# A gated scan and top-1 MoE: the last two unconditional tiles' scatters stand behind the conditional parts

## The chip, the cores and the metric

The kernel runs on one core of a Trainium2 chip. The metric is the device time of one execution in microseconds (us). The engines are PE (matmuls; PEld is its weight load), DVE, ACT, POOL and SP. Here SP starts the loads and the gathers, POOL the indirect scatters. A "q" behind an engine's name (POOLq) means its sequencer: branches, semaphores, drains and the issue of DMAs.

## The reference

Four sequences of 5056 tokens with 256 channels go through a gated scan over time; the result, 20224 tokens, goes through a mixture of 8 experts, of which each token takes one.

```python
# B, S, D = 4, 5056, 256;  N = 20224;  E, F = 8, 1024
f = lower_bound + (1.0 - lower_bound) * sigmoid(f_logit)
for t in range(S):
    h = f[:, t] * h + (1 - f[:, t]) * x[:, t]
    y[:, t] = h
x = y.reshape(B * S, D)
e_idx = argmax(x @ w_gate, axis=1)
gate_w = softmax(x @ w_gate)[arange(N), e_idx]
eom = sigmoid(x @ w_output_gate)
for e in range(E):
    mask = e_idx == e
    ye = maximum(x[mask] @ w1[e], 0.0) @ w2[e]
    out[mask] = gate_w[mask, None] * eom[mask, e, None] * ye
```

## The kernel before

**Chunks.** The tokens go through the scan in 40 chunks of 512, channels on the partitions. `chunk()` is a generator; each `yield` ends a stage. In their order: the tanh on ACT (L265), (f - 1) x on DVE (L269), the scan on DVE (L280), squares on ACT (L287) and their sum on PE (`pv`, L291). From that sum `pow2` works out a power of two as a scale, in five DVE instructions on a 128x1 tile (L142, L144, L146, L148, L150: `xv`, `xs`, `xi`), each of which reads what the one ahead wrote; L296 and L299 make of it `sa` and `li`. With `sa` ACT writes the high f16 half of the result (L310) and DVE the low half (L314); SP turns both from channels to rows with transposing DMAs (L307), after which PE computes the gate logits (L329). The routing on DVE (L372 to L421: `oh`, `og`, `gs`, `pos`, `eg`) gives every token its place, and POOL scatters the rows, two f16 halves and the gate's factor, into `scr`, sorted by expert (L433).

**Weights.** The weights of each expert come in two halves, 16 in all. Each is loaded by SP (L566), bounded by a gram on PE (L578), a norm on DVE (L585) and a sum on PE (L592), scaled by the same five instructions of `pow2` (names with w), and split into a high half by ACT (L614) and a low one by DVE (L619, into `w1s` and `w2s`).

**First tiles.** While the weights arrive, 16 tiles of 128 rows, one per expert after chunk 3 and one after chunk 5, are gathered and computed (matmuls L715 to L717 and L735 to L737, relu on ACT, its low half `el` on DVE in L726). They use separate code because the expert is known in advance. What ends with the last of them, at about 184 us of the trace, is called the front part below.

**Tiles.** Then `experts()` computes tiles of sorted rows: 64 of 256 rows, and up to 37 more of 128 rows, as many as the routing has filled. 18 of the 37 always run, so that 82 tiles (0 to 81) are unconditional; the other 19 stand in two conditional parts, 3 behind `used > 18` and 16 behind `used > 21`. `used` is loaded in L964 from a count that the routing left; each `tc.If` (L966) becomes a branch on every engine. In the traced execution neither body runs.

A tile is gathered by SP with a transposing DMA (`xq`, L630) and a small load with its rows' factors and places (`mt`, L633). DVE copies the expert's first weights (L657), PE does the first product (L669 to L671), ACT the relu (L674), DVE the low half (L682), and PE the second product (L702 to L704). ACT writes the scaled result to `yo` (L746, two buffers), and `put` scatters it to the output with one indirect DMA on POOL per 128 rows (L750). The loop overlaps three tiles: in turn t it gathers tile t + 1, does the first product of t and the second of t - 1, and evacuates and scatters t - 2. At the border to the conditional parts the gather of the next tile (82) is issued ahead, in case they run. The chunks that are left run between the quarters of a tile, one stage at a time.

**Order.** The instructions are written in one program order, and the compiler's scheduler, which works with its own timeline, may move what does not depend on each other. `ordered(start, cut)` limits this: it walks the list and ties each instruction to the one ahead on the same engine. Instructions ahead of index `cut` on DVE, ACT, PE and POOL are left free; SP is always tied. The index `prog["cut"]` is taken where the front part ends.

```python
for i, ins in enumerate(nc.cur_bb.bb.instructions[start:]):
    free = i < cut and ins.engine in loose
    if ins.engine in prev and not free:
        tc.add_manual_dep(ins, prev[ins.engine], AFTER, reason="order")
    prev[ins.engine] = ins.name
```

So the front part is in SP's order as written, and in the scheduler's on the other four engines; all that follows stands as written. The program's end is L1003.

Of the kernel before, what the change touches and what calls it, by code (L numbers as in the profile page):

```python
# [8 lines left out]
F32 = mybir.dt.float32  # L9
# [3 lines left out]
I16 = mybir.dt.int16  # L13
# [32 lines left out]
def raw(ins):  # L46
    return getattr(ins, "ins", ins)
# [3 lines left out]
def tile_scan_moe(  # L51
# [11 lines left out]
    P = 128  # L63
    D, N = xT.shape
# [27 lines left out]
    gp = ctx.enter_context(tc.tile_pool(name="gp", bufs=3))  # L92
# [104 lines left out]
    def apart(ins, group, keep=()):  # L197
        tc.declare_no_dep(raw(ins), group=group, keep=[raw(k) for k in keep], reason="rows apart")
        tc.add_to_no_dep_group(group, raw(ins))
# [422 lines left out]
    mpool = {}  # L622

    def gather(t, slot, e=None):
        tab, j, nb, new = slot
        n = nb * P
        r = nc.sync.value_load(tab[j : j + 1, 0:1], min_val=0, max_val=FREE + P - n)
        xq = gp.tile([P, 2, KD, 256], I16, tag="xq", name="xq")
        mt = gp.tile([P, 2, 4], I16, tag="mt", name="mt", bufs=4)
        i1 = nc.sync.dma_start_transpose(  # L630
            out=xq.rearrange("p a k n -> p (a k) n")[:, :, 0:n], in_=scr[ds(r, n), 0 : 2 * D]
        )
        i2 = nc.sync.dma_start(out=mt[:, 0:nb, :], in_=scr[ds(r, n), CM : CM + 4].rearrange("(b p) d -> p b d", p=P))  # L633
        for ins in (i1, i2):
            for k in new:
                tc.add_manual_dep(raw(ins), raw(k).name, DATA, reason="rows scattered")
            apart(ins, "scr", new)
        return dict(xh=xq[:, 0].bitcast(F16), xl=xq[:, 1].bitcast(F16), mt=mt, nb=nb, tab=tab, j=j, id=t, ev=e)
# [100 lines left out]
    def evacuate(T):  # L739
        nb = T["nb"]  # L740
        if isinstance(T["ev"], int):
            T["yo"] = yo = ep.tile([P, 1, D], F32, tag="ey", name="ey", bufs=2)
        else:
            T["yo"] = yo = mpool["m"].tile([P, 2, D], F32, tag="yo", name="yo", bufs=2)
        for b in range(nb):
            nc.scalar.activation(yo[:, b, :], T["y"][:, b, :], AF.Copy, scale=T["fac"][:, b : b + 1])  # L746

# [6 lines left out]
            apart(ins, "out")  # L754


    prog = {"begun": 0, "tick": 0, "done": 0, "left": 0.0, "planned": 0, "final": False, "got": 0, "rounds": 0}
    live = []
    total = sure(N)
    tail = (N - 256 * total + E * (P - 1)) // P  # L760
# [54 lines left out]
    tiles = {}  # L815
# [95 lines left out]
    def ordered(start, cut):  # L911

        loose = [e.engine for e in (nc.vector, nc.scalar, nc.tensor, nc.gpsimd)]
        prev = {}
# [3 lines that stand above are left out]
                tc.add_manual_dep(ins, prev[ins.engine], AFTER, reason="order")  # L918
            prev[ins.engine] = ins.name

    def experts(t0, t1, more):
        ahead(t0)
        alone(expert(tiles[t0]))
        alone(fetch1(tiles[t0], 0))
        for t in range(t0, t1 + 2):
            T = tiles.get(t) if t < t1 else None
            U = tiles.get(t - 1) if t0 < t <= t1 else None
            V = tiles.get(t - 2) if t > t0 + 1 else None
            rate = RATE * (T or U or V)["nb"] / 2
            for q in range(4):  # L930
                tasks = []
                if q == 0:
                    if t + 1 < t1 + min(more, 1):
                        ahead(t + 1)
                    if T:
                        tasks.append(fetch1(T, 1))
                elif q == 2:
                    if t + 1 < t1:
                        alone(expert(tiles[t + 1]))
                        tasks.append(fetch1(tiles[t + 1], 0))  # L940
                elif q == 3 and T:
                    tasks.append(factors(T))
                if q == 0 and U:
                    tasks.append(low(U, 3))
                if q and T:
                    tasks.append(low(T, q - 1))
                step(rate, tasks)
                if q == 0 and V:
                    evacuate(V)
                if q == 1 and V:  # L950
                    put(V)
                if T:
                    gemm1(T, q)
                if U:
                    gemm2(U, q)

    cuts = [n for n in MORE if n < tail] + [tail]
    between["on"] = True
    experts(0, total + cuts[0], len(cuts) - 1)
    beside()  # L960
    ordered(0, prog["cut"])

    if len(cuts) > 1:
        used = nc.values_load(prog["count"][0:1, 0:1], min_val=0, max_val=tail)  # L964
        for a, b in zip(cuts[:-1], cuts[1:]):
            with tc.If(used > a):  # L966
                experts(total + a, total + b, 0)
                ordered(0, 0)


# [36 lines left out]
```

## Time and profile before

| | |
|---|---|
| time, median of 3 runs | 989.14 us (987.89 to 991.45) |
| time of the profiled execution | 990.77 us |
| its span / mean granted clock of PE | 989.1 us / 0.988 |
| busy: PE, DVE, ACT, POOL | 907.7, 801.0, 519.7, 390.1 us |
| first matmul of tile 0 (L669) | 184.5 us |

The span runs from the first to the last instruction of the profiled execution; 1.7 us of its time lie outside. Times in the rows are counted from the span's start. A row of the timeline has the start, the duration, the engine, line and operation with what it writes and reads, a count (x2: a second one follows), and in brackets the idle time ahead of it and what ended that. A row of a group ends with the idle time ahead of its instructions.

### The profile page before, as it was taken

How to read it: one execution, taken by the hardware profiler on the slowest of the kernel's cores; microseconds unless marked ns; L12 is line 12 of the kernel's file. 1: busy time of each engine (PE TensorE's matmuls, PEld its weight loads, DVE VectorE, ACT ScalarE, POOL GpSimd, SP SyncE). 2: the span in 40 equal slices, each digit the busy share in tenths (PEclk: the TensorE clock that was granted, in tenths of full speed). 3: DMA queues.
4: the chain of work that ended last, by engine and by line, in shares of the span. 5: the costliest groups of instructions: out<-in, count | busy, mean ns of one | idle time of the engine just before them, and what ended most of it. 6: DMA issues, size and time to landing. Idle time of an engine off the chain costs nothing. (4 is left out here: it accounts for less than half of the span.)

```text
span 989.1 us, 30907 instructions
## 1 busy us (share of the span) xinstructions
PE 907.7 (92%) x9775; PEld 819.7 (83%) x9775; DVE 801.0 (81%) x2639; ACT 519.7 (53%) x1075; POOL 390.1 (39%) x378
## 2 busy tenths in 40 slices
PE   2258898899999999999999999999999999999993
PEld 2247887788888888888888888888888888899992
DVE  7989897888989988888898888888888886545550
ACT  6667675555555555555565555555555543333331
POOL 1432334434445454454545434455444443211111
PEclk9999999999999999999999999999999999999997
DMA  8899984855575657556576665655666544312120
GB/s 310 206 275 293 237 230 126 188 157 151 131 157 144 151 153 167 141 133 152 150 153 150 169 138 140 153 148 157 150 163 134 129 100 90 100 45 43 41 57 17
DMA packets 238558, 146.56 MB, mean 148 GB/s; under 512 B 202557, under 2 KB 204223, under 8 KB 238400
## 3 DMA queue, kind: packets, MB, share of 16 engines
q1 hardware_dynamic: 222752, 101.74, 44.9%
q0 software_dynamic: 15360, 42.74, 14.4%
q8 instruction: 95, 1.56, 0.7%
q14 instruction: 63, 0.52, 0.2%
q10 hardware_dynamic: 288, 0.02, 0.0%
HBM read 58.38 MB, written 44.49 MB: 104 GB/s over the span
## 5 line engine op out<-in xcount | busy, mean ns | idle before, releaser
L674 ACT ACTIVATE hh<-ph 128x512 f16<-128x512 f32 (+1 forms) x328 | 180.4, 550 | 307.8 <-PE ph L671 297.4
L669 PE MATMUL ph<-xq,w 128*128 128x256 f16 (+1 forms) x1312 | 330.4, 260 | 2.9 <-DMA xq<-scr 2.4
L671 PE MATMUL ph<-xq,w 128*128 128x256 f16 (+1 forms) x1312 | 331.1, 261 | 0.0
L670 PE MATMUL ph<-xq,w 128*128 128x256 f16 (+1 forms) x1312 | 330.9, 261 | 0.0
L750 POOL DMA_INDIRECT out_dram<-yo,mt x146 | 175.3, 1201 | 363.2 <-ACT yo L746 339.9
L704 PE MATMUL py<-w2s,hl 128*128 x1168 | 318.5, 273 | 0.0
L703 PE MATMUL py<-w2s,hh 128*128 x1168 | 318.4, 273 | 0.0
L702 PE MATMUL py<-w2s,hh 128*128 x1168 | 318.1, 272 | 0.0
L682 DVE SCALAR_TENSOR_TENSOR hl<-ph,hh 128x512 f16<-128x512 f32 (+1 forms) x328 | 204.9, 625 | 58.2 <-ACT hh L674 55.8
L433 POOL DMA_INDIRECT scr<-rows,dst x154 | 175.7, 1141 | 122.6 <-issue 109.3
L657 DVE COPY w<-w1s 128x2048 f16 x164 | 120.3, 734 | 35.1 <-PE ph L671 33.3
L669 PEld LDWEIGHTS <-w 128*128 128x128 f16 x1312 | 127.9, 98 | 14.3 <-DVE fac L649 2.7
L671 PEld LDWEIGHTS <-w 128*128 128x128 f16 x1312 | 128.0, 98 | 11.9
L670 PEld LDWEIGHTS <-w 128*128 128x128 f16 x1312 | 127.9, 97 | 9.7
L704 PEld LDWEIGHTS <-hl 128*128 128x128 f16 x1168 | 114.1, 98 | 13.8
L702 PEld LDWEIGHTS <-hh 128*128 128x128 f16 x1168 | 114.0, 98 | 11.4
L703 PEld LDWEIGHTS <-hh 128*128 128x128 f16 x1168 | 113.9, 98 | 10.6
L280 DVE TENSOR_TENSOR_SCAN xt<-ft,xt 128x512 f32<-128x512 f32 (+4 forms) x78 | 90.8, 1172 | 0.0
L746 ACT ACTIVATE yo<-py,fac 128x256 f32<-128x256 f32 x146 | 61.8, 468 | 26.7 <-PE py L704 26.1
L314 DVE SCALAR_TENSOR_TENSOR ft<-xt,sa,ft 128x512 f16<-128x512 f32 (+1 forms) x76 | 56.2, 744 | 20.1 <-ACT ft L265 18.3
L329 PEld LDWEIGHTS <-ft 128*128 128x128 f16 x600 | 51.7, 99 | 15.1 <-ACT ft L310 4.9
L310 ACT ACTIVATE ft<-xt,sa 128x512 f16<-128x512 f32 (+1 forms) x76 | 50.2, 707 | 23.3 <-DVE li L299 16.0
(171 smaller groups left out, 1298.7 us busy)
## 6 DMA issues: line engine op xcount, KB each, us to landing
ft<-in_fT_dram SPq DMA_DIRECT2D x37, 512.0 KB
xt<-in_xT_dram SPq DMA_DIRECT2D x37, 512.0 KB
w<-in_wT_dram SPq DMA_DIRECT2D x32, 512.0 KB
scr<-rows,dst POOLq DMA_INDIRECT x154
rows<-ft SPq DMA_TRANSPOSE x152
out_dram<-yo,mt POOLq DMA_INDIRECT x146
xq<-scr SPq DMA_TRANSPOSE x99
scr<-padt SPq DMA_DIRECT2D x9, 136.0 KB
```

The lines of the kernel that those rows point to most:

```text
L280: nc.vector.tensor_tensor_scan(out=xt[:, k, a:z], data0=ft[:, k, a:z], data1=xt[:, k, a:z], initial=init, op0=ALU.mult, op1=ALU.add)
L433: ins = nc.gpsimd.indirect_dma_start(out=scr[:, :], out_offset=IOA(ap=dst[:, b : b + 1], axis=0), in_=rows[:, b, :], in_offset=None)
L657: nc.vector.tensor_copy(out=w, in_=w1f[:, ds(T["ev"] * (2 * WH) + h * 2 * QH, 2 * QH)])
L669: nc.tensor.matmul(out=o, lhsT=w[:, f, k, 0, :], rhs=T["xh"][:, k, 0:n], start=first, stop=False)
L670: nc.tensor.matmul(out=o, lhsT=w[:, f, k, 0, :], rhs=T["xl"][:, k, 0:n], start=False, stop=False)
L671: nc.tensor.matmul(out=o, lhsT=w[:, f, k, 1, :], rhs=T["xh"][:, k, 0:n], start=False, stop=last)
L674: nc.scalar.activation(hh[:, :, 0:n], ph[:, :, 0:n], AF.Relu)
L682: nc.vector.scalar_tensor_tensor(out=hl[:, :, 0:n], in0=ph[:, :, 0:n], scalar=0.0, in1=hh[:, :, 0:n], op0=ALU.max, op1=ALU.subtract)
L702: nc.tensor.matmul(out=o, lhsT=hh[:, i, c], rhs=wh, start=first, stop=False, skip_group_check=True)
L703: nc.tensor.matmul(out=o, lhsT=hh[:, i, c], rhs=wl, start=False, stop=False, skip_group_check=True)
L704: nc.tensor.matmul(out=o, lhsT=hl[:, i, c], rhs=wh, start=False, stop=last, skip_group_check=True)
L750: ins = nc.gpsimd.indirect_dma_start(out=out[:, :], out_offset=IOA(ap=T["mt"][:, b, 2:4].bitcast(I32), axis=0), in_=T["yo"][:, b, :], in_o ...
```

## The change

It has three parts.

- `mt` and `yo` of the conditional tiles get tags of their own (`mtc`, `yoc`; two buffers each).
- `experts` for the 82 unconditional tiles runs with `more` = 0: the gather of tile 82 is no longer issued ahead of the border.
- With `late` = 2 it leaves out `put` for tiles 80 and 81. They are scattered after both conditional parts, and a last `ordered(0, 0)` ties what now stands at the end of the block. Since it walks the block's whole list and with `cut` = 0, it also ties the front part's instructions on DVE, ACT, PE and POOL.

```diff
@@ gather
-        mt = gp.tile([P, 2, 4], I16, tag="mt", name="mt", bufs=4)
+        tag = prog["places"]
+        mt = gp.tile([P, 2, 4], I16, tag="mt" + tag, name="mt" + tag, bufs=2 if tag else 4)
@@ evacuate
-            T["yo"] = yo = mpool["m"].tile([P, 2, D], F32, tag="yo", name="yo", bufs=2)
+            tag = prog["places"]
+            T["yo"] = yo = mpool["m"].tile([P, 2, D], F32, tag="yo" + tag, name="yo" + tag, bufs=2)
...
-    def experts(t0, t1, more):
+    def experts(t0, t1, more, late=0):
...
-                if q == 1 and V:
+                if q == 1 and V and t - 2 < t1 - late:
                     put(V)
...
-    experts(0, total + cuts[0], len(cuts) - 1)
+
+    end = total + cuts[0]
+    late = min(2, end) if len(cuts) > 1 else 0
+    experts(0, end, 0, late)
     beside()
     ordered(0, prog["cut"])
+    prog["places"] = "c"
 
     if len(cuts) > 1:
         used = nc.values_load(prog["count"][0:1, 0:1], min_val=0, max_val=tail)
@@
             with tc.If(used > a):
                 experts(total + a, total + b, 0)
                 ordered(0, 0)
+    for t in range(end - late, end):
+        put(tiles[t])
+    ordered(0, 0)
```

POOL, the end of the program, before (L750 is the scatter, L964 the load of the count, L966 the conditions):

```order
L750 DMA out_dram<-yo,mt 20224x256 x28
L964 TENSOR_LOAD pl_count
L966 COMPARE_AND_BRANCH
L750 DMA out_dram<-yo,mt 20224x256 x3
L966 UNCONDITIONAL_BRANCH
L966 ISA
L966 UNCONDITIONAL_BRANCH
L966 COMPARE_AND_BRANCH
L750 DMA out_dram<-yo,mt 20224x256 x16
```

And after, where the lines have the numbers 752, 970 and 972:

```order
L752 DMA out_dram<-yo,mt 20224x256 x26
L970 TENSOR_LOAD pl_count
L972 COMPARE_AND_BRANCH
L752 DMA out_dram<-yoc,mtc 20224x256 x3
L972 UNCONDITIONAL_BRANCH
L972 ISA
L972 UNCONDITIONAL_BRANCH
L972 COMPARE_AND_BRANCH
L752 DMA out_dram<-yoc,mtc 20224x256 x16
L972 UNCONDITIONAL_BRANCH
L972 ISA
L972 UNCONDITIONAL_BRANCH
```

Two of the 28 scatters ahead of the load are gone there; they follow behind the last of these rows, ahead of the program's end.

DVE, in the front part (some 147 us into the trace of before), where `xv_2706` to `xi_2708` are the five links of one chunk's scale; before:

```order
L142 TENSOR_SCALAR xv_2706<-pv_2652 128x1
L726 SCALAR_TENSOR_TENSOR el_2632<-ph_2572,eh_2597 128x512
L375 TENSOR_TENSOR og_2648<-oh_2646,lgo_2625 128x32
L600 SCALAR_TENSOR_TENSOR cinv_94<-wi_2392,wi_2554 128x1
L619 SCALAR_TENSOR_TENSOR w2s_127<-w_2221,ws_2553,w2s_127 128x4x256
L144 TENSOR_SCALAR xv_2706<-xv_2706 128x1
L378 TENSOR_REDUCE gs_2650<-og_2648 128x4
L619 SCALAR_TENSOR_TENSOR w2s_127<-w_2223,ws_2553,w2s_127 128x4x256
L269 SCALAR_TENSOR_TENSOR xt_2629<-ft_2628,xt_2629 128x512
L403 TENSOR_TENSOR pos_2779<-pk_2695,cnt_2233 128x32
L409 TENSOR_TENSOR cnt_2785<-cnt_2233,pk_2695 128x8
L269 SCALAR_TENSOR_TENSOR xt_2629<-ft_2628,xt_2629 128x512
```

The same place after (L727 is L726 of before):

```order
L372 TENSOR_TENSOR oh_2646<-key_2641,km_2644 128x32
L375 TENSOR_TENSOR og_2648<-oh_2646,lgo_2625 128x32
L378 TENSOR_REDUCE gs_2650<-og_2648 128x4
L142 TENSOR_SCALAR xv_2706<-pv_2652 128x1
L619 SCALAR_TENSOR_TENSOR w2s_127<-w_2221,ws_2553,w2s_127 128x4x256
L144 TENSOR_SCALAR xv_2706<-xv_2706 128x1
L727 SCALAR_TENSOR_TENSOR el_2709<-ph_2656,eh_2681 128x512
L146 TENSOR_SCALAR xv_2706<-xv_2706 128x1
L148 TENSOR_SCALAR xs_2707<-xv_2706 128x1
L150 TENSOR_SCALAR xi_2708<-xs_2707 128x1
L296 TENSOR_SCALAR sa_2717<-na_101,xs_2707 128x2
L299 TENSOR_TENSOR li_2719<-xi_2708,gi4_121 128x1
```

Before, 26 rows lie from the chain's first link to its last, which comes 15 rows below the end of the piece shown; after, six, with one L619 and one L727 among them. The two L269 and the four scans (L280) that stood between its links now come behind it.

More of the change, by code (lines that the diff above doesn't have):

```diff
@@ L754, in put @@
             apart(ins, "out")
-    prog = {"begun": 0, "tick": 0, "done": 0, "left": 0.0, "planned": 0, "final": False, "got": 0, "rounds": 0}
+    prog = {"places": "", "begun": 0, "tick": 0, "done": 0, "left": 0.0, "planned": 0, "final": False, "got": 0, "rounds": 0}
     live = []
```

## The prediction

> **What bounds the kernel now.** The page's head first: one execution with a span of 989.1 us, PE busy for 92% of it.
>
> ```profile
> span 989.1 us, 30907 instructions
> PE 907.7 (92%) x9775; PEld 819.7 (83%) x9775; DVE 801.0 (81%) x2639; ACT 519.7 (53%) x1075; POOL 390.1 (39%) x378
> ```
>
> An average hides stages, so the busy times by stretch come next (columns: length, PE, weight loads, DVE, ACT, POOL, granted clock, DMA share, GB/s), with the row of the tiles' first matmul, whose start (184.5) marks the end of the front part.
>
> ```profile
> 60.00:80.00 20.00, 16.06 (x202) 15.19 (x202) 15.70 (x59) 12.19 (x21) 7.64 (x9) 1.00 1.08 319
> 80.00:100.00 20.00, 15.17 (x216) 13.75 (x214) 19.25 (x57) 13.84 (x23) 3.73 (x4) 1.00 1.12 254
> 100.00:120.00 20.00, 18.99 (x271) 18.36 (x272) 17.79 (x58) 15.45 (x28) 6.96 (x6) 0.91 1.00 240
> 120.00:140.00 20.00, 17.80 (x275) 16.59 (x273) 17.74 (x56) 13.61 (x25) 8.84 (x10) 1.00 0.91 254
> 140.00:160.00 20.00, 19.36 (x266) 17.90 (x264) 18.21 (x57) 14.84 (x27) 5.28 (x6) 1.00 0.42 107
> ...
> 400.00:500.00 100.00, 100.00 (x1003) 89.63 (x1002) 89.59 (x284) 55.33 (x114) 50.26 (x44) 1.00 0.62 149
> L669 PE MATMUL ph<-xq,w x1312: 219/272/374, 184.5 to 968.7; 128*128 128x256 f16 x147, 128*128 128x128 f16 x41
> ```
>
> From 184.5 to the last tile PE is the bound: it has no idle time in the row 400 to 500. What moves the first tile's start moves the end by as much, and no other engine's saving in between counts. In the front part no engine is full: from 60 to 160 DVE is busy for 15.70 + 19.25 + 17.79 + 17.74 + 18.21 = 88.7 of 100 us, PE for 87.4. There the order of the instructions decides.
>
> Then the end, since PE's last matmul row is over 20 us before the span's end. The timeline's last scatters and evacuation, and the sequencers' rows of three lines: L964 loads the count, L966 is the two conditions, L1003 the program's end (columns: count, shortest/median/longest ns, first and last start).
>
> ```profile
> 965.18 0.98 POOL L750 DMA_INDIRECT out_dram<-yo,mt  x1 [4.32 <-ACT yo L746]
> 970.48 0.98 POOL L750 DMA_INDIRECT out_dram<-yo,mt  x1 [4.32 <-ACT yo L746]
> 972.80 0.47 ACT L746 ACTIVATE yo<-py,fac 128x256 f32<-128x256 f32 x1 [2.59 <-PE py L704]
> 973.55 0.98 POOL L750 DMA_INDIRECT out_dram<-yo,mt  x1 [2.08 <-ACTq L966]
> ...
> L964 POOLq TENSOR_LOAD <-pl_count x1: 501/501/501, 973.3 to 973.3; - x1
> L966 PEldq COMPARE_BRANCH  x2: 3852/4162/4472, 972.9 to 977.1; - x2
> L966 POOLq COMPARE_BRANCH  x2: 45/45/45, 973.9 to 976.5; - x2
> L966 POOLq INC_SWDGE_SEM  x2: 2322/2328/2335, 974.2 to 977.0; - x2
> L1003 SPq EVENT_SEMAPHORE  x14: 17/28/2154, 979.3 to 989.0; - x14
> L1003 POOLq EVENT_SEMAPHORE  x4: 17/17/17, 988.3 to 989.0; - x4
> L1003 POOLq DRAIN  x3: 40/107/8885, 979.4 to 988.8; - x3
> L1003 SPq DRAIN  x3: 7/7/13, 982.2 to 988.5; - x3
> L1003 PEldq DRAIN  x2: 8/8/8, 981.9 to 988.7; - x2
> ```
>
> POOL ends last. It passes the two conditions only after its last scatter: 973.9 the first, an increment of 2.33 us, 976.5 the second, another increment, and at 979.4 a drain of 8.885 us, over at 988.3; the barrier takes the other 0.8. PE, with two branches of 3.9 and 4.5 us, is there at 981.9 and SP at 982.2: 6.1 us before POOL.
>
> **The change, part by part.** *The end.* POOL meets the conditions two scatters earlier. After the third-last scatter (965.18 + 0.98 = 966.2) come the load (0.50) and two branches and increments, which took 974.1 to 979.4, 5.3 us: done by about 972. Meanwhile the next scatter, ready at about 970.5, waits 1.5 us; nobody waits for it, as both buffers of the last two tiles are used once more and never again. The last scatter is ready when its evacuation ends, 972.80 + 0.47 = 973.3, and over at 974.5 at the latest. Then the drain: 974.5 + 8.9 = 983.4, + 0.8 = 984.2. This gains 989.1 - 984.2 = **4.9 us**. The ends: PE's branches stay, so SP is not through before 982.2, + 0.8 = 983.0, a gain of 6.1, if the drain only waited for the increments; if it ends a fixed 13.8 us after the last scatter (988.3 - 974.5), nothing. I take 4.9, the drain as long as its row, behind POOL's last work. A loss has no mechanism here: every moved instruction stands on POOL alone, which waited 4.32 us before each of these scatters.
>
> *No gather across the border, and the separate places.* One transposing gather and one small load less on SP, for a tile that does not run here; PE has no idle time left by it. Zero, both ways. The new tags are used only inside the conditional parts, which are skipped: zero.
>
> *The last call of ordered.* It walks the list of the whole main part again, with no free stretch. So the front part, up to 184 us, whose DVE, ACT, PE and POOL instructions a scheduler had ordered, now stands as written. SP's order is unchanged there, so its rows show where the front part is held up. The longest stop: a transpose (L307) waits from 149.95 to 158.05 for ACT's L310, which needs a chain of five small DVE instructions (L142 to L150) of one chunk and the scale behind them. The gather behind the transpose (161.89) is what PE then waits for.
>
> ```profile
> 145.92 1.24 SPq L630 DMA_TRANSPOSE xq<-scr  x1
> 149.57 0.38 SPq L633 DMA_DIRECT2D mt<-scr  x1
> 158.05 2.99 SPq L307 DMA_TRANSPOSE rows<-ft  x2
> 161.89 1.24 SPq L630 DMA_TRANSPOSE xq<-scr  x1
> ...
> 147.13 0.15 DVE L142 TENSOR_SCALAR xv<-pv 128x1 f32<-128x1 f32 x1
> 147.19 0.68 DVE L726 SCALAR_TENSOR_TENSOR el<-ph,eh 128x512 f16<-128x512 f32 x1
> 147.96 1.28 DVE L619 SCALAR_TENSOR_TENSOR w2s<-w,ws,w2s 128x1024 f16<-128x1024 f32 x1
> 149.15 0.15 DVE L144 TENSOR_SCALAR xv<-xv 128x1 int32<-128x1 int32 x1
> 151.88 0.15 DVE L146 TENSOR_SCALAR xv<-xv 128x1 int32<-128x1 int32 x1
> 153.43 0.15 DVE L148 TENSOR_SCALAR xs<-xv 128x1 f32<-128x1 f32 x1
> 156.70 0.15 DVE L150 TENSOR_SCALAR xi<-xs 128x1 int32<-128x1 int32 x1
> 157.32 1.32 ACT L310 ACTIVATE ft<-xt,sa 128x512 f16<-128x512 f32 x2
> 164.74 0.23 PE L715 MATMUL ph<-xq,w1s 128*128 128x128 f16 x1 [3.26 <-DMA xq<-scr]
> ```
>
> The chain starts at 147.13 and ends 9.6 us later, because the scheduler put other work between its links. As written, one L619 (1.28) and one L726 (0.68) stand in it: 147.13 + five links of 0.19 + 1.28 + 0.68 + the scale's 0.2 = 150.2, 7.0 us earlier. Not all of it arrives: the work that stood between (two L269, four scans) goes behind and belongs to the next chunk, whose transpose SP reaches soon after. Ends: 7.0 and 0; I take **5 us gained**, nearer to the 7.0, as all that follows on SP are gathers that PE waits for.
>
> Against it stands the price of the written order. Links of a chain now often stand next to each other: over the front part's 528 DVE instructions I count 106 neighbours of which the second reads what the first wrote, 29 before. A row early in the trace shows what that costs:
>
> ```profile
> 17.99 0.16 DVE L142 TENSOR_SCALAR xv<-pv 128x1 f32<-128x1 f32 x1 [0.18 <-PE pv L291]
> 18.07 0.15 DVE L299 TENSOR_TENSOR li<-xi,gi 128x1 f32<-128x1 f32 x1
> 18.18 0.15 DVE L144 TENSOR_SCALAR xv<-xv 128x1 int32<-128x1 int32 x1
> 18.38 0.15 DVE L146 TENSOR_SCALAR xv<-xv 128x1 int32<-128x1 int32 x1
> ```
>
> An independent one starts 0.08 us after the one ahead (17.99 to 18.07) and leaves its neighbour where it was; a dependent one starts 0.20 after (18.18 to 18.38). So 77 more pairs cost some 0.10 us each, 7.7 us of DVE time. DVE has 11 idle us in the 100 from 60 to 160 that can take part of it: I take half, **4 us lost**. Ends for all that the written order does beside the stop above: DVE's share there falls to the 80% of 60:80's PE (16.06 of 20), 88.7/0.80 = 110.9, a loss of 10.9; or its idle time shrinks, a gain of 3 (a third of the 11.3).
>
> The Trainium skill, "VectorE: DVE Perf Modes", section "The DRAIN you can't avoid", says that the next operation does not start until the pipe is empty, and that a semaphore between two costs nothing extra. By that rule neighbours would cost the same whether they depend on each other or not, and the term would be 0 instead of 4. The rows above speak against it here: 0.08 against 0.20 us.
>
> **The sum.** 989.1 - 4.9 - 5 + 4 = 983.2. The profiled execution took 990.77 with its span of 989.1, and the median of the runs is 989.14; a difference of 5.9 us from that median gives **983.2 us**. A measurement of this kernel tells about 0.3% (3 us) from no change.
>
> **Rivals.** (1) *The front part loses more than the end gains.* Engines that take their work as written wait at the head of the queue: a norm (L585) waits for PE's gram, PE for a gather, with ready work behind both. For it: DVE, PE and DMA are all near 90% from 80 to 140, so one waiting engine soon stops the others. Against it: from 400 to 500 everything stands as written too, and PE never waits, DVE at 89.59. Its price is the 10.9 with the stop not shortened: 989.1 - 4.9 + 10.9 = 995. It decides once the written order costs more than the 4.9 (7.9 for slower by 0.3%). (2) *The end gains nothing*, because POOL's drain counts from the last scatter: 989.1 - 5 + 4 = 988. For it: the scatter is the last real work on that queue; against it: the increments lie between and the last bytes are sent long before 988. (3) *The front part moves nothing* (another stop takes the place of the 8 us one): 984.2. (4) *The written order costs nothing*, as by the page's rule, or DVE's idle time takes all of it, and the stop goes whole: 989.1 - 4.9 - 7 = 977.
>
> **How the numbers follow.** The forecast has 0.40, (1) 0.18, (2) 0.12, (3) 0.15, (4) 0.15. Faster: nearly all of the forecast (0.36), (3), (4) = 0.66; the same: (2) and the forecast's edge, 0.16; slower: (1), 0.18. The range reaches from below (4), where the idle time shrinks too (977 - 3 = 974, and 1 for the drain's better end), to (1): 973 to 996. The forecast's own range, from its bounds: 977 to 988.
>
> **What would show it.** The end: POOL's increments start near 967 instead of 974.2, its last drain near 974.5, PE's two branches stay at 3.9 and 4.5 us, and the span ends 11 to 12 us after the last evacuation (972.80 before) instead of 16. The front: SP's stop before L307 near 150 is down to about 1 us, and the tiles' first matmul starts at 183.5 (184.5 - 5 + 4). If that start is over 192, rival (1) holds; if the drain starts early but still ends 13.8 us after the last scatter, (2). What would make the prediction wrong is above all the front part: hundreds of instructions change places and two terms of opposite sign were priced from a few rows.

## The result and the profile after

The changed kernel takes 999.28 us (median of 4 runs, 998.76 to 1001.29) against 989.41 us of the kernel before on the same chip (4 runs): a ratio (of the means) of 1.0102, 95% interval 1.0078 to 1.0126. It is slower; 983.2 (973 to 996) was forecast. The page's head of the profiled execution after:

```profile
span 997.8 us, 30891 instructions
PE 910.9 (91%) x9775; PEld 821.3 (82%) x9775; DVE 803.4 (81%) x2639; ACT 518.6 (52%) x1075; POOL 397.9 (40%) x378
```

The engines do the same work as before within 1 to 2% (POOL's spans are rough). The span is 8.7 us longer (997.8 - 989.1) and PE, which bounds the kernel, is busy for 3.2 us more, so the larger part is waiting. First the end: the timeline's last evacuation and scatters, and the sequencers' rows of the conditions (L972) and of the program's end (L1012).

```profile
978.67 0.98 POOL L752 DMA_INDIRECT out_dram<-yo,mt  x1 [4.32 <-ACT yo L748]
985.61 0.98 POOL L752 DMA_INDIRECT out_dram<-yo,mt  x1 [5.95 <-DMA out_dram<-yo,mt]
987.03 0.98 POOL L752 DMA_INDIRECT out_dram<-yo,mt  x1 [0.44 <-ACTq L972]
...
986.28 0.47 ACT L748 ACTIVATE yo<-py,fac 128x256 f32<-128x256 f32 x1 [2.58 <-PE py L705]
...
L972 POOLq INC_SWDGE_SEM  x2: 2284/2301/2318, 979.6 to 982.4; - x2
L1012 POOLq DRAIN  x3: 40/113/10110, 986.8 to 997.5; - x3
L1012 SPq DRAIN  x3: 7/7/13, 995.8 to 997.2; - x3
L1012 PEldq DRAIN  x2: 8/8/8, 995.6 to 997.2; - x2
```

This part went as worked out. POOL passes the conditions (979.6 to 984.7) while the last two tiles are still computed, and its last scatter follows the last evacuation at once. Its drain ends at 986.8 + 10.1 = 996.9, which is 8.9 us after that scatter's end (988.0), as long as the drain of before. From the end of the last evacuation (986.75) to the end of the span it is 11.0 us; before it was 15.8 (973.27 to 989.1). The end gained 4.8 us.

Then the front part: the busy times by stretch (the columns of the prediction's), and the row of the tiles' first matmul.

```profile
60.00:80.00 20.00, 15.58 (x202) 13.71 (x202) 19.43 (x66) 14.55 (x25) 7.01 (x6) 1.00 1.05 279
80.00:100.00 20.00, 11.62 (x149) 10.38 (x147) 16.97 (x56) 13.92 (x22) 8.21 (x6) 0.79 0.72 181
100.00:120.00 20.00, 18.32 (x260) 17.16 (x258) 14.60 (x49) 10.52 (x19) 5.76 (x4) 0.96 0.98 247
120.00:140.00 20.00, 15.04 (x215) 14.15 (x216) 16.66 (x58) 13.25 (x25) 4.33 (x6) 1.00 0.96 274
140.00:160.00 20.00, 16.15 (x226) 15.31 (x225) 18.59 (x47) 12.52 (x21) 9.38 (x8) 0.91 0.67 155
160.00:180.00 20.00, 20.00 (x266) 18.39 (x265) 15.17 (x46) 11.11 (x24) 8.52 (x7) 0.92 0.50 102
...
L670 PE MATMUL ph<-xq,w x1312: 219/272/421, 199.2 to 982.2; 128*128 128x256 f16 x147, 128*128 128x128 f16 x41
```

The tiles begin at 199.2 instead of 184.5, 14.7 us later. From there to the last evacuation's end it takes 787.5 us against 788.8. So the account is +14.7 - 1.2 - 4.8 = +8.7. In these 120 us PE is busy for 96.7 us, 104.1 before. The stretch that lost most is 80 to 100 (11.62 against 15.17), where the granted clock is down to 0.79 too (no run tells apart what that costs by itself); from 120 to 160 another 6.0 us are missing (31.2 against 37.2).

What PE waits for from 80 to 100 is a gather of the first tiles (the fourth), and that waits for the scatters of chunk 4 (chunks are counted from 0). The path of chunk 4 in the timelines, before: the end of its scale chain on DVE, its first and last scatter on POOL, the gather on SP, the first matmul behind it on PE.

```profile
53.16 0.15 DVE L299 TENSOR_TENSOR li<-xi,gi 128x1 f32<-128x1 f32 x1
77.16 0.97 POOL L433 DMA_INDIRECT scr<-rows,dst  x1 [2.84 <-issue]
81.52 0.96 POOL L433 DMA_INDIRECT scr<-rows,dst  x1 [0.30 <-issue]
86.50 1.23 SPq L630 DMA_TRANSPOSE xq<-scr  x1
91.30 0.22 PE L715 MATMUL ph<-xq,w1s 128*128 128x128 f16 x1 [1.55 <-DMA xq<-scr]
```

And after:

```profile
59.24 0.15 DVE L299 TENSOR_TENSOR li<-xi,gi 128x1 f32<-128x1 f32 x1
84.08 1.79 POOL L433 DMA_INDIRECT scr<-rows,dst  x1 [4.33 <-issue]
89.76 1.82 POOL L433 DMA_INDIRECT scr<-rows,dst  x1 [0.30 <-issue]
93.19 1.25 SPq L631 DMA_TRANSPOSE xq<-scr  x1
95.91 0.27 PE L716 MATMUL ph<-xq,w1s 128*128 128x128 f16 x1 [6.14 <-DMA xq<-scr]
```

The chunk is 6 us late at its scale and 7 to 8 at its scatters. SP, which takes its work as written, waits ahead of the gather until 87.4 for a table from DVE (`pf_tab`, the gather's place) and from 88.1 to 93.1 for these scatters to land, and PE for 6.14 us behind it. At that matmul PE is 4.6 us late (95.91 against 91.30), a third of the 14.7.

The other two thirds come later. These are rows of the changed kernel: three steps of chunk 8 (its sum, behind PE's longest gap from 120 to 160, its scale and its gates), and the gather and DVE's copy of weights that tile 0 waits for; then scale and gates of chunk 8 before.

```profile
157.15 0.16 PE L291 MATMUL pv<-hss,na 128*128 128x1 bf16 x1 [3.40 <-ACT ft L287]
162.34 0.15 DVE L299 TENSOR_TENSOR li<-xi,gi 128x1 f32<-128x1 f32 x1
173.71 0.35 PE L329 MATMUL pr<-wgs,ft 128*128 128x32 f16 x8
194.36 1.27 SPq L631 DMA_TRANSPOSE xq<-scr  x1
198.42 0.69 DVE L658 COPY w<-w1s 128x2048 f16 x1 [1.02 <-issue]
...
156.98 0.26 DVE L299 TENSOR_TENSOR li<-xi,gi 128x1 f32<-128x1 f32 x1
158.26 0.18 PE L329 MATMUL pr<-wgs,ft 128*128 128x32 f16 x1
```

Ahead of 157.15 PE stands 3.4 us for chunk 8's squares (L287), with matmuls of a first tile right behind. Chunk 8 is 5.4 us late at its scale but 15.4 at its gates: ACT's L310 starts 2.9 us behind the scale (0.3 before), and then the chunk stands behind the first tiles' matmuls, with PE busy for all of 160 to 180. PE is through with the first tiles at 194.7 (184.1 before, 10.6 us late). Then it waits for tile 0: the gather, which chunk 8's scatters hold, has landed at 198.9, and DVE's copy is over at 199.1. Before, that gather had landed at 182.6, ahead of PE.

### The profile page after: what moved, and what is told of

Its sections match the earlier page's. It is cut to its first block, busy times and chain, and to the rows that moved or that the text cites. A ratio compares the mean times of both kernels' runs of the same rounds, so it can differ in the third digit from the quotient of the medians.

```text
span 997.8 us, 30891 instructions
## 1 busy us (share of the span) xinstructions
PE 910.9 (91%) x9775; PEld 821.3 (82%) x9775; DVE 803.4 (81%) x2639; ACT 518.6 (52%) x1075; POOL 397.9 (40%) x378
## 3 DMA queue, kind: packets, MB, share of 16 engines
q0 software_dynamic: 15360, 42.74, 14.2%
## 4 chain that ended last, share of the span: by engine, by line
PE 72%; DVE 9%; issue 7%; DMA 7%; POOL 2%; ACT 1%; SPq 1%; POOLq 0%; DVEq 0%; ACTq 0%
PE ph L670 11%; PE py L703 11%; PE ph L671 11%; PE ph L672 11%; PE py L704 11%; PE py L705 11%; DMA out_dram<-yo,mt 3%; DMA xq<-scr 2%; POOL out_dram L752 1%; DVE xt L280 1%; DVE w1s L619 1%; PE pr L329 1%; DVE w2s L619 1%; PE ph L716 1%; PE ph L718 1%
## 5 line engine op out<-in xcount | busy, mean ns | idle before, releaser
L752 POOL DMA_INDIRECT out_dram<-yo,mt x146 | 170.9, 1170 | 361.3 <-ACT yo L748 328.5
L433 POOL DMA_INDIRECT scr<-rows,dst x154 | 189.3, 1230 | 136.7 <-issue 117.9
L658 DVE COPY w<-w1s 128x2048 f16 x164 | 117.3, 715 | 34.7 <-PE ph L672 32.9
L704 PEld LDWEIGHTS <-hh 128*128 128x128 f16 x1168 | 113.9, 97 | 10.6
L280 DVE TENSOR_TENSOR_SCAN xt<-ft,xt 128x512 f32<-128x512 f32 (+4 forms) x78 | 90.6, 1172 | 0.3 <-ACT ft L274 0.3
L314 DVE SCALAR_TENSOR_TENSOR ft<-xt,sa,ft 128x512 f16<-128x512 f32 (+1 forms) x76 | 56.1, 742 | 20.6 <-ACT ft L265 18.0
L310 ACT ACTIVATE ft<-xt,sa 128x512 f16<-128x512 f32 (+1 forms) x76 | 50.2, 708 | 30.3 <-DVE li L299 24.0
L274 ACT ACTIVATE ft<-ft,fb,fa 128x512 f32<-128x512 f32 (+1 forms) x76 | 57.3, 799 | 6.4 <-DVE xt L269 4.2
```

Source lines behind the costliest of these rows:

```text
L280: nc.vector.tensor_tensor_scan(out=xt[:, k, a:z], data0=ft[:, k, a:z], data1=xt[:, k, a:z], initial=init, op0=ALU.mult, op1=ALU.add)
L433: ins = nc.gpsimd.indirect_dma_start(out=scr[:, :], out_offset=IOA(ap=dst[:, b : b + 1], axis=0), in_=rows[:, b, :], in_offset=None)
L658: nc.vector.tensor_copy(out=w, in_=w1f[:, ds(T["ev"] * (2 * WH) + h * 2 * QH, 2 * QH)])
L704: nc.tensor.matmul(out=o, lhsT=hh[:, i, c], rhs=wl, start=False, stop=False, skip_group_check=True)
L752: ins = nc.gpsimd.indirect_dma_start(out=out[:, :], out_offset=IOA(ap=T["mt"][:, b, 2:4].bitcast(I32), axis=0), in_=T["yo"][:, b, :], in_o ...
```

## The experiments

The comparisons ran on several chips; every ratio is to the kernel before on the same chip, which took 989 to 990 us in three comparisons (that of the result; e5 to e8; s1 and s2) and 1005 to 1012 in three (e1 to e4; e9 to e12; r1 to r4). Starts within a trace are compared within a comparison, or with the trace of before where before took 989 us: the front part in the same order ended at 184.5 there and at 192.3 in e1.

### Each part alone: e1, e2

e1 is the changed kernel with this edit:

```diff
     for t in range(end - late, end):
         put(tiles[t])
-    ordered(0, 0)
+    ordered(0, prog["cut"])
```

> The changed kernel with its last ordered(0, prog["cut"]) instead of ordered(0, 0): the front part keeps the scheduler's order, only the end of the program is changed. If the end gains what the two traces show between the last evacuation's end and the span's end (15.8 us before, 11.0 changed), this takes 989.4 - 4.8 = 984.6, with the tiles' first matmul at 184.5. If the gain of the end needed the later arrival of the other engines and is lost here, 988 to 990.

e2 is the kernel before with the opposite one:

```diff
     beside()
-    ordered(0, prog["cut"])
+    ordered(0, 0)
```

> The kernel before with its ordered(0, prog["cut"]) replaced by ordered(0, 0): the front part in the written order on all engines, the end as before. If the front part alone carries the loss: first matmul of the tiles near 199, time 989.4 + 14.7 = 1004. If the loss came from something else in the change (the gather that is no longer issued, the tags), 989 to 992.

Measured: e1 0.9944 (0.9922 to 0.9966), e2 1.0171 (1.0137 to 1.0204), with the tiles' first matmul at 192.3 and 211.7. The end alone gains what the traces show; the front part's order alone carries the whole loss, 1.6% (e1 to the changed kernel) to 1.7% (e2). e1 beats both kernels.

### One engine at a time: e3, e5, e6, e8, e4

`ordered` takes the list of engines that are left to the scheduler in the front part; the last call of the changed kernel becomes

```diff
-    ordered(0, 0)
+    ordered(0, prog["cut"], (nc.tensor,))                          # e3
+    ordered(0, prog["cut"], (nc.vector,))                          # e5
+    ordered(0, prog["cut"], (nc.scalar, nc.tensor, nc.gpsimd))     # e6
+    ordered(0, prog["cut"], (nc.tensor, nc.vector))                # e8
```

> The changed kernel with PE alone left to the scheduler in the front part; DVE, ACT and POOL stay in the written order. Theory A (PE in the written order waits for a gather at the head of its queue, with the chunks' small sums and gates behind it): most of the 14.7 us comes back, the tiles' first matmul stands at 185 to 190, time 985 to 990. Theory B (DVE in the written order stops and falls behind with the weights): the first matmul stays at 196 to 200, time 996 to 1000.

> The changed kernel with DVE alone left to the scheduler in the front part; PE, ACT and POOL in the written order. Theory B (DVE in the written order stands idle early, 32.6 of 20 to 60 us busy against 37.1, takes the weights' low halves later, and so delivers chunk 4's scale at 59.2 instead of 53.2; the first tiles' fourth gather and PE follow): the scale of chunk 4 is back near 53, that gather near 87, and 60% or more of the loss comes back: with the end's gain the time is 0.995 to 1.002 of before. Theory A (PE's head of queue): 1.006 to 1.012 of before. Theory C (no one engine: each one's head of queue costs a third): 1.004 to 1.007.

> The changed kernel with only DVE in the written order in the front part; PE, ACT and POOL are left to the scheduler. Theory B: the loss stays, 1.005 to 1.011 of before, chunk 4's scale still near 59. Theories A and C: 0.996 to 1.003.

> The changed kernel with PE and DVE left to the scheduler in the front part, ACT and POOL in the written order. Theories A, B and C all expect most of the loss back here: 0.995 to 1.001 of before. If it stays above 1.004, ACT's or POOL's order carries a part of its own (ACT ran chunk 7's tanh at 112.6 instead of 99.1).

e4 leaves only the two matmuls of each chunk's `pv` (L291) out of the tie (`sums` holds their names):

```diff
-            free = i < cut and ins.engine in loose
+            free = i < cut and ins.engine in loose or ins.name in sums
...
-            prev[ins.engine] = ins.name
+            if ins.name not in sums:
+                prev[ins.engine] = ins.name
```

> The changed kernel with only the chunks' sums (pv, L291, two matmuls of one column each per chunk) out of the tie on PE; all else in the written order. Theory A in its narrow form (the sum of the chunk in work stands behind the first tiles' matmuls: pv of chunk 6 ran at 102.3, its squares were done at 93.8): half of the loss or more comes back, time 988 to 993. Theory B: 996 to 1000.

Measured: e3 1.0060 (1.0036 to 1.0084), e5 1.0139 (1.0118 to 1.0160), e6 1.0104 (1.0081 to 1.0126), e8 1.0106 (1.0084 to 1.0128), e4 1.0095 (1.0068 to 1.0122). Theories A and B both fall, as neither PE's order nor DVE's is needed for the loss: with DVE alone left free it stays (e5), with PE alone only a part comes back (e3). But one engine is enough: DVE alone in the written order (e6) costs as much as all four, and so do ACT and POOL without DVE and PE (e8). Taking the sums out of PE's row (e4) brings nothing back that this tells. (The scheduler orders the free engines anew each time, so these kernels differ in more than the tie.) What they have in common stands in this table, read from the timelines (us):

| | ratio | chunk 4: scale | last scatter | fourth gather | chunk 8: last scatter | tiles' first matmul |
|---|---|---|---|---|---|---|
| before | 1 | 53.2 | 81.5 | 86.5 | 175.5 | 184.5 |
| after | 1.0102 | 59.2 | 89.8 | 93.2 | 191.4 | 199.2 |
| e1 end only | 0.9944 | 53.5 | 81.8 | 86.8 | 181.0 | 192.3 |
| e2 front only | 1.0171 | 60.0 | 92.6 | 96.0 | 204.0 | 211.7 |
| e3 PE free | 1.0060 | 59.0 | 92.1 | 96.1 | 194.1 | 201.8 |
| e4 pv free | 1.0095 | 59.9 | 91.0 | 94.5 | 199.9 | 207.6 |
| e5 DVE free | 1.0139 | 52.1 | 88.5 | 91.1 | 197.5 | 204.5 |
| e6 only DVE tied | 1.0104 | 58.9 | 91.5 | 96.0 | 193.6 | 201.6 |
| e7 dst x4 | 1.0098 | 55.9 | 89.7 | 93.1 | 188.8 | 196.6 |
| e8 PE, DVE free | 1.0106 | 54.7 | 89.1 | 95.0 | 193.0 | 200.8 |
| e9 first third free | 1.0052 | 53.1 | 79.4 | 84.9 | 190.7 | 198.5 |
| e10 first third tied | 1.0101 | 59.3 | 94.8 | 97.8 | 200.8 | 207.0 |
| e12 late = 1 | 0.9983 | 53.4 | 80.5 | 85.6 | 180.6 | 191.4 |

Where an engine is tied early in the written order, chunk 4's last scatter comes at 88.5 to 94.8; where none is, at 79.4 to 81.8. That holds even where the scale is on time again (e5, 52.1): the next queue on the chunk's way holds it. The gates (L329) of chunk 4 ran at 64.3 there as in the changed kernel, 54.7 before, behind the matmuls of a first tile that PE had waited for (7.54 us in e5).

### The stop of DVE: e7

In the changed kernel's trace DVE stands 3.30 us at 39.9 for a tile (`dst`) that a scatter still reads.

```diff
-        dst = small("dst", None, I32)
+        dst = sp.tile([P, NB], I32, tag="dst", name="dst", bufs=4)
...
-        es = small("es")
+        es = km
```

> The changed kernel, all in the written order, but the places' tile (dst, written by L416 on DVE) has four buffers instead of two, and es takes over the dead tile km to make room. In the changed kernel's trace DVE stands 3.30 us at 39.9 before L416 because the scatter two chunks back still reads that tile. Theory B in its narrow form (that stop starts the lateness): the stop is gone, chunk 4's scale moves up by 2 to 3 us and the time by 2 to 5 us, 1.006 of before where the changed kernel has 1.010. If the stop is only moved to the next instruction that waits for the same scatter, or eaten by later waits: 1.009 to 1.012.

Measured: 1.0098 (1.0076 to 1.0121). The stop is gone and the scale moved up by 3.3 us (59.2 to 55.9), but the last scatter by 0.1 only. The stop was no cause.

### Which third: e9, e10

`prog["mid"]` is the index where the loop over the weights' halves reaches 6; in e10 `ordered` takes a third argument, the index from which instructions are left free.

```diff
-    ordered(0, 0)
+    ordered(0, prog["mid"])                  # e9: free up to there, then tied
+    ordered(0, prog["cut"], prog["mid"])     # e10: tied up to there, then free to the cut
```

> The changed kernel with the front part's first third (up to the weights' half 6, which takes in chunk 4's scatters) left to the scheduler, the rest of it in the written order. Theory D (the loss is made early: chunk 4's scatters come at 84 to 88 in every kernel with a tied engine, 77 with none, and the first tiles' fourth gather and PE wait for them): scatters at 77 to 79, that gather at 87 to 89, time 0.994 to 0.999 of before. Theory E (the written order loses along the whole front part): 1.001 to 1.006. Theory F (the loss is made behind half 6): 1.006 to 1.011.

> The opposite: the first third in the written order, the rest of the front part left to the scheduler. Theory D: scatters of chunk 4 at 84 or later, 1.006 to 1.012 of before. Theory E: 1.001 to 1.006. Theory F: 0.994 to 0.999.

Measured: e9 1.0052 (1.0029 to 1.0074), e10 1.0101 (1.0064 to 1.0137). The early third alone costs as much as the whole; the later two thirds alone cost 1.1% over e1 as well: chunk 4 is on time there, but chunk 8's last scatter stands at 190.7, where e12 of the same comparison has 180.6. The two do not add up to more than the whole; why they overlap was not tried.

### A delay that was none: e11

On e1:

```diff
         nc.vector.reciprocal(out=fc[:, 0:nb], in_=fc[:, 0:nb])
+        if c == 4:
+            for _ in range(16):
+                nc.gpsimd.affine_select(
+                    out=fc[:, 0:nb], in_=fc[:, 0:nb], pattern=[[1, nb]], compare_op=ALU.is_ge, fill=0.0, base=0,
+                    channel_multiplier=1,
+                )
```

> The kernel of the end alone (the front part as the scheduler has it), with 16 selections on POOL that change no value put between L428 and L430 of chunk 4, so that its scatters come later by what they take; by the shortest rows of POOL (an iota of one column, 0.13) 2 to 4 us. Nothing else is delayed, the weights' halves least of all. Theory D: the fourth gather comes later by the same 2 to 4, and the tiles' first matmul by at least as much: 0.9944 becomes 0.997 to 1.000. If chunk 4's lateness is only a sign, and what costs is the weights' halves that came late in the same kernels (the first low half at 45 to 53 instead of 30.5): 0.993 to 0.996.

Measured: 0.9964 (0.9939 to 0.9989). The selections took their time (L430 of chunk 4 came at 76.4, in e12 at 69.6), but the scatters also wait for the places that DVE writes (`dst`, at 75.5 in e12 and no later here). So the first and the last of them stood at 77.0 and 81.9, where e12 of the same comparison has 76.4 and 80.5. It decides nothing.

### The scheduler's order as a table: r1 to r4, s1, s2

For these the order that the scheduler gave the front part's 530, 196, 1652 and 92 instructions on DVE, ACT, PE and POOL was written into the changed kernel as a table in place of its last call, and each engine tied in that order. `ROWS` holds the table, packed, as the distance by which each entry moves; `extra` holds instructions that a run adds, which go ahead of the one that they are noted for:

```diff
-    ordered(0, 0)
+    body = nc.cur_bb.bb.instructions
...
+    for key, eng in named.items():
+        at = array.array("h")
+        at.frombytes(zlib.decompress(base64.b85decode(ROWS[key])))
+        mine = [x for x in body[: prog["cut"]] if x.engine == eng.engine and x.name not in extra]
+        rest = [x for x in body[prog["cut"] :] if x.engine == eng.engine]
+        row = []
+        for i, d in enumerate(at):
+            x = mine[i + d]
+            row += [y for y in body if extra.get(y.name) == x.name and y.engine == eng.engine]
+            row.append(x)
+        row += rest
+        for p, x in zip(row[:-1], row[1:]):
+            tc.add_manual_dep(x, p.name, AFTER, reason="order")
```

> The kernel of the end alone, but the front part's DVE, ACT, PE and POOL instructions are tied in the very order that the scheduler gave them before, by a table. If the order is what costs, and tying by itself costs nothing: 0.994 of before, as the kernel of the end alone. If instructions that are tied lose something of their own (more waits between neighbours): 1.000 or more.

Measured: 0.9950 (0.9925 to 0.9974), as e1 within the intervals: a tie by itself costs nothing that this tells, the order does. Now one thing can be moved while every other queue keeps its order. (The traced execution of r1 took 995.40 us against a median of 1000.68, those of r3 and r4 1004.04 and 1003.15 against 1001.69 and 998.81; starts that differ by a few us between these traces are weighed by the ratios.) r2 puts 20 selections that keep every element ahead of chunk 4's scatters in POOL's row:

```diff
+        held = []
+        for _ in range(20 if c == 4 else 0):
+            fcm = meta[:, :, 0:2].bitcast(F32)
+            held.append(raw(nc.gpsimd.affine_select(
+                out=fcm, in_=fcm, pattern=[[1, nb], [0, 1]], compare_op=ALU.is_ge, fill=0.0, base=0, channel_multiplier=1,
+            )).name)
         for b in range(nb):
             ins = nc.gpsimd.indirect_dma_start(
...
             fresh.append(ins)
+            if b == 0:
+                extra.update({k: raw(ins).name for k in held})
```

> The replayed order with 20 selections on POOL, which change no value, between L430 and the scatters of chunk 4; in the run before 8 of them took 2.99 us, so 20 hold the scatters and what follows on POOL by 7.5 us, and nothing else can move. Theory D (chunk 4's lateness is what costs): the scatters come at 84 to 85, the fourth gather at 93 to 95, and the tiles' first matmul 7 to 15 us later than in r1: 1.001 to 1.009 of before. If the front part takes the delay up again before its end: 0.994 to 0.998.

Its timeline, and the row of the tiles' first matmul:

```profile
74.05 11.12 POOL L447 TENSOR_SCALAR_AFFINE_SELECT rows<-rows 128x4 f32<-128x4 f32 x20
85.45 1.83 POOL L451 DMA_INDIRECT scr<-rows,dst  x1 [0.28 <-DVE wv L157]
90.12 0.96 POOL L451 DMA_INDIRECT scr<-rows,dst  x1 [0.30 <-issue]
92.68 1.24 SPq L651 DMA_TRANSPOSE xq<-scr  x1
95.45 0.26 PE L736 MATMUL ph<-xq,w1s 128*128 128x128 f16 x1 [4.19 <-DMA xq<-scr]
...
L690 PE MATMUL ph<-xq,w x1312: 219/272/282, 197.2 to 989.3; 128*128 128x256 f16 x147, 128*128 128x128 f16 x41
```

And that row in r1:

```profile
L682 PE MATMUL ph<-xq,w x1312: 219/272/283, 189.8 to 978.2; 128*128 128x256 f16 x147, 128*128 128x128 f16 x41
```

Measured: 1.0016 (0.9994 to 1.0039), 0.66% above r1. The first scatter comes 10.4 us later than in r1 (75.1), the gather 8.5 (84.2), the tiles 7.4. So the lateness of chunk 4's scatters is a cause, with no other queue's order changed: nothing behind it makes up for all of it. (What POOL does next, a first tile's output and the next chunk's iota, comes 9 us later with them; the 4.19 us that PE stands are for the gather.)

r3 moves four entries of DVE's row (each row of these two diffs is an entry of the table, by its line):

```diff
-L619 half 0
-L619 half 0
...
-L619 half 1
-L619 half 1
...
+L619 half 0
+L619 half 0
+L619 half 1
+L619 half 1
 L142 chunk 4
```

> The replayed order, with only the first four low halves of the weights (L619 of halves 0 and 1) moved on DVE from 28 to 48 us to the place ahead of chunk 4's chain at 52, where the written order has two of them and the other two just behind. DVE's work stays the same, 4 x 1.28 = 5.1 us of it are done later. Theory D: chunk 4's scale comes at 58 to 59 instead of 53.2, its scatters 4 to 5 us later, and the time is 0.998 to 1.005 of before. If a single engine's late work is taken up by the other engines' free time: 0.994 to 0.997.

Measured: 0.9955 (0.9931 to 0.9979), the same as r1: the scale came 2.6 us later (56.2), the last scatter 2.1, and the time shows nothing. So the weights' low halves done later are not what costs 1.6%. For chunk 4 this run says little: at r2's rate its 2.1 us would make 0.13%, which these intervals can't show.

r4 does the one thing that the prediction counted on, in DVE's row (and in ACT's, where L310 of chunk 8 moves up behind L265 of chunk 9):

```diff
 L142 chunk 8
 L726
+L144 chunk 8
 L375
+L146 chunk 8
 L600
+L148 chunk 8
+L378
+L150 chunk 8
+L296 chunk 8
+L299 chunk 8
 L619
-L144 chunk 8
-L378
 L619
...
+L314 chunk 8
+L314 chunk 8
 L280 chunk 9
```

> The replayed order with the one change that the prediction hoped for: chunk 8's scale chain (L144 to L150, L296, L299) stands together behind L142, ACT's L310 of that chunk ahead of the next chunk's L274, and DVE's L314 ahead of the next chunk's scan. By the prediction's term the stop of SP before L307 (149.95 to 158.05 before) falls to 1 to 2 us, the gather behind it comes 6 to 7 us earlier, and the tiles' first matmul 5 us: 0.989 of before. If that matmul hangs on chunk 8's scatters, which have waits of their own on the plan of the tiles: 0.992 to 0.995.

SP's rows of the transposes of chunk 8 (L319 there) and the gather behind them, in r1 and then in r4:

```profile
161.09 3.28 SPq L319 DMA_TRANSPOSE rows<-ft  x2
165.67 0.97 SPq L643 DMA_TRANSPOSE xq<-scr  x1
```

```profile
153.34 2.98 SPq L319 DMA_TRANSPOSE rows<-ft  x2
157.15 1.22 SPq L643 DMA_TRANSPOSE xq<-scr  x1
```

The stop is down from 9.5 us (r1) to 1.2 and the gather is 8.5 us earlier, but PE finishes the first tiles at 190.3 (189.3 in r1), the tiles' first matmul stands at 190.8 (189.8), and the ratio is 0.9937 (0.9911 to 0.9962). That is 0.13% under r1, 1.3 us, and by the two intervals uncertain by some 0.35%: no difference that this tells, and the 5 us that were counted on lie just outside. Chunk 8's last scatter stayed where it was (180.8 against 179.6). PE's gap of 2.9 us ahead of the gathered tile (165.81 to 168.74 in r1) is gone; the same time went into gaps of 1.2 and 1.3 us within the next tile's matmuls, of which the trace shows no cause (r1's has four of that kind elsewhere, at 135.6 to 138.5 and 181.7); that stays open.

s1 and s2 are r2 with other numbers:

```diff
-        for _ in range(20 if c == 4 else 0):
+        for _ in range({4: 14, 8: 16}.get(c, 0)):     # s1
+        for _ in range({8: 16}.get(c, 0)):            # s2
```

> The replayed order with 14 selections on POOL ahead of chunk 4's scatters and 16 ahead of chunk 8's; 20 took 11.1 us in r2, so 7.8 and 8.9 us. They change no value. If the lateness of these two chunks is the whole loss (chunk 4 holds the first tiles' fourth gather and PE, chunk 8 the tiles' first gather): the tiles' first matmul 13 to 16 us later than in r1 (189.8), 1.008 to 1.011 of before, as the changed kernel. If chunk 4's delay makes room that chunk 8's then uses: 1.000 to 1.005, and the rest of the loss lies elsewhere, on PE's queue.

> The replayed order with the 16 selections ahead of chunk 8's scatters alone. The tiles' first gather comes 8 to 9 us later (182.4 in r1), behind the last of the first tiles' matmuls; the tiles' first matmul follows it by 7 us: 1.001 to 1.004 of before. If PE has other work to fill that time (it has none that I see in its queue, which stands as a row): 0.995 to 0.999.

Measured: s1 1.0038 (1.0020 to 1.0055), s2 0.9989 (0.9970 to 1.0008). Over r1 (0.9950, on another chip) that is 0.9% and 0.4%: both delays cost, and s1 lies in the second of the expected ranges, the one that leaves a rest to PE's queue: a little over half of the 1.6%. The delays came out smaller than planned, those of chunk 8 above all: its 16 selections took 5.3 and 5.1 us instead of 8.9, and POOL had stood idle there (5.4 us in r1). s1's row:

```profile
172.63 5.29 POOL L447 TENSOR_SCALAR_AFFINE_SELECT rows<-rows 128x4 f32<-128x4 f32 x16 [2.72 <-DVE rows L442]
```

Against the trace of before, chunk 8's last scatter is 7.1 us late in s1 (182.6) and the first matmul 6.0 (190.5); in s2 4.4 (179.9) and 3.4 (187.9); in the changed kernel 15.9 and 14.7. In these three the tiles' first matmul follows that scatter by 8 us, and the gather lands within 0.3 us of it. Before and in r1 it follows by 9 and 10 us, with PE through with the first tiles only 0.5 us ahead of it: there the scatter doesn't hold it. That the order makes the rest of the 1.6% in the same way is inferred from e9, e10 and chunk 8's rows above; no run delays the two chunks by the full amount.

### One scatter instead of two: e12

```diff
-    late = min(2, end) if len(cuts) > 1 else 0
+    late = min(1, end) if len(cuts) > 1 else 0
```

on e1. 

> The kernel of the end alone with late = 1: only the scatter of tile 81 stands behind the conditions. By the model of the prediction (POOL's load, branches and increments take 5.3 us from the end of the last scatter ahead of them, then the last scatter, then a drain of 8.9 us and 0.8 for the barrier) POOL is through the conditions at 971.5 + 5.3 = 976.8, the last scatter at 977.8, the end at 987.5: a gain of 1.6 us, 0.998 of before, where late = 2 has 0.9944. If the gain comes from anything that is the same for one and two (the conditions no longer behind the very last scatter): 0.994 to 0.996.

Measured: 0.9983 (0.9959 to 1.0007), as worked out. Its last evacuation, last scatter and POOL's drain:

```profile
995.10 0.47 ACT L748 ACTIVATE yo<-py,fac 128x256 f32<-128x256 f32 x1 [2.56 <-PE py L705]
...
999.48 0.98 POOL L752 DMA_INDIRECT out_dram<-yo,mt  x1 [5.68 <-DMA out_dram<-yo,mt]
...
L1012 POOLq DRAIN  x3: 40/113/10100, 999.3 to 1009.9; - x3
```

The scatter comes 3.9 us after the evacuation's end, the drain is over 8.9 us after the scatter's (1000.46 to 1009.4), the span 14.6 us after the evacuation; 14.2 was worked out (15.8 less 1.6).

## Why the prediction was wrong

- **The end, 4.9 us**: right, 4.8 by the traces, 0.56% in e1. The drain starts when POOL's last work is done and lasts its 8.9 us; rival (2) is out. PE and SP were through at 995.6 and 995.8, ahead of POOL's 996.9, as the sum had it; so no more than 1.1 us are left to gain there. (The "over 20 us" ahead of it was read off the first products' row, which starts last at 968.7. PE's last matmul ends at 972.7, 16.4 us before the end; no term hangs on it.)
- **The gather and the places, 0**: right; e1 has both and only the end's gain.
- **The shortened stop, 5 us gained**: this step failed. The stop fell (from 8.1 to 4.4 us in the changed kernel, from 9.5 to 1.2 in r4), but it was not on the path. The sum took "all that follows on SP are gathers that PE waits for" as enough; in r4 the gather came 8.5 us earlier and PE was through with the first tiles no earlier, and the tiles' first gather hangs on chunk 8's scatters.
- **The price of the written order, 4 us lost, and its upper end of 10.9**: this is the step that made the result wrong. It priced neighbours on DVE. DVE's busy time rose by 2.4 us in all (801.0 to 803.4), and 5 us of DVE's work done later cost nothing that r3 can tell. The order cost 14.7 us, on a path that the sum never followed: one chunk's scale, gates, logits, routing and scatters pass DVE, ACT, PE, DVE and POOL, a queue tied in the written order holds them behind work that waits for something else, and the next gather waits for the last scatter. That this path costs is shown (r2, s1, s2), for 0.9 of the 1.6%; that the rest is made on it too is inferred. The bound of 10.9 came from one engine's share in one stretch, so it was no bound. The forecast's "977 to 988" are rivals (4) and (2) and not the sum of its terms' ends, which reach to 1000; 999.3 lies below that by chance, as the end did gain.
- **Rival (1)** is what happened: engines wait at the head of their queues, PE for a gather, with ready work behind. Its sign and its kind were right, its price (10.9, so 995) too small, and its chance of 0.18 looks low: the row 80 to 140, with three resources near 90%, spoke for it, and the argument against it was drawn from 400 to 500, where each gather is issued a tile ahead.

## What to carry to other kernels

A call that ties an order must be read by its range: the gain of 0.56% at the end was real, and the second walk over the whole list cost nearly three times as much. To price a new order, follow one item through every queue that it passes, to the wait that holds the engine that bounds, and compare the places of that item in each queue; costs of neighbours on one engine say little. An order that a scheduler found can be written down as a table, and then single delays can be tested with no other queue's order changed. A delay that is made of instructions has to be read off its own trace: the same selections were planned at 8.9 us and took 5.1.

## What the runs showed of the hardware

POOL's last drain was over 8.9 us after POOL's last work in four kernels, whether that was an increment (979.4 to 988.3 before) or a scatter (988.0 to 996.9 after, 996.5 to 1005.4 in e1, 1000.5 to 1009.4 in e12). A condition that was not taken held PE's sequencer for 3.7 to 4.7 us (3.9 and 4.5 before, 3.7 and 4.7 after), and POOL's for a branch of 0.05 us and an increment of 2.3.

A selection of 128x4 elements on POOL, each reading what the one ahead wrote, took 0.20 to 0.24 us in 13 of r2's 20 and 0.54 to 1.25 in the other seven. Each of the seven began while DVE ran an instruction that reads two tensors of the on-chip memory (L619, L269, L314 or L280), and ended within 0.1 us of that instruction's end or of the next one like it. Beside `el` (L726), which reads PE's output, a selection kept its 0.20. So 20 took 11.1 us in r2, and 16 took 5.3 and 5.1 in s1 and s2 at chunk 8.
